# Cross-covariance attention with a gated feed-forward block: longer q-k bursts, an uneven last output tile, and a later second v tile

## Chip, cores, metric

One core of one Trainium2 chip. The metric is the device time of one execution in microseconds (us), the median of several runs. No second state of the chip is in play: all runs quoted here are of the state called fast.

## The reference

For each of 4 batches of 6016 tokens and 256 channels, channel attention makes a 256 x 256 matrix from normalized q and k, applies it to v, and a feed-forward block with a silu gate (256 to 1536 to 256) follows:

```python
def _attn_ref(q, k, v, tau):
    qn = q / (np.linalg.norm(q, axis=1, keepdims=True) + 1e-06)
    kn = k / (np.linalg.norm(k, axis=1, keepdims=True) + 1e-06)
    s = kn.transpose(0, 2, 1) @ qn / tau
    s = s - s.max(-1, keepdims=True)
    a = np.exp(s)
    a /= a.sum(-1, keepdims=True) + 1e-09
    return (v @ a).astype(np.float32)

def _moe_ref(x, w_gate, w_val, w_out):
    g = x @ w_gate
    silu = g * (1.0 / (1.0 + np.exp(-g)))
    val = x @ w_val
    return (silu * val @ w_out).astype(np.float32)
```

## The kernel before

The attention matrix is multiplied into w_gate and w_val once per batch (`Wg`, `Wv`), so that v goes straight into the feed-forward block. v comes in chunks of 512 rows; a chunk has 12 steps, and in each TensorE makes `g_ps` and `v_ps` for this chunk and two `o_new` matmuls for the one before. While one batch runs, q and k of the next are loaded, squared and multiplied in the background: `plan[step]` lists what is issued at a step. A v tile is loaded by GpSimd's queue, which casts it, into a buffer in DRAM, and SyncE's queue transposes it from there into `vT`:

```python
    def load_v(b, ci):
        ...
        vb = vb_tiles[(b * NCH + ci) % 2]
        nc.gpsimd.dma_start(
            out=vb[:mv, :].rearrange("(p s) c -> p (s c)", s=cm),
            in_=v[b, cs * P:cs * P + mv, :].rearrange("(p s) c -> p (s c)", s=cm))

    def transpose_v(b, ci):
        ...
        nc.sync.dma_start_transpose(out=vT[:, :, :mv], in_=vb[:mv, :])

    def gemm1_pair(b, t):            # the q-k product of two row blocks, fp8
        ...
        for jh in range(CH):
            js = slice(jh * P, (jh + 1) * P)
            if pm == 2:
                nc.tensor.matmul(kq[:, jh, :], q_sb[:, ps:ps + 2, js],
                                 k_sb[:, ps:ps + 2, :],
                                 start=(t == 0 and jh == 0), stop=last,
                                 perf_mode=DR, skip_group_check=True)
        ...
    # make_plan(b): two pairs at a time
            plan[step].append((norm_acc, t))
            if t % 2 == 1:
                plan[step + 1].append((gemm1_pair, t - 1))
                plan[step + 1].append((gemm1_pair, t))
    # the start, after all of batch 0's k and q; one queue, in this order
    load_first_v()
    load_w(0, HW)                    # HW = 256, WP = 512
    load_w(HW, WP)
    load_v(*allc[1])
    transpose_v(*allc[1])
    for wc in range(1, NWC):
        load_w(wc * WP, (wc + 1) * WP)
    nc.gpsimd.dma_start(out=w_out_sb, ...)
```

`load_w` loads one block of columns of w_gate and one of w_val. Behind w_out follow, in the same queue, the third v tile and the first q and k of batch 1. The end of the kernel (`finish`) makes the last 128 output rows in two halves of 128 columns, each in a tile of the pool `psum_o`, which has two.

## Time and profile before

| | before |
|---|---|
| time, median of 3 runs | 811.15 us (810.33 to 811.29) |
| same kernel, beside the changed one, 6 runs | 810.77 us (810.26 to 811.29) |
| span of the profiled run | 808.5 us |
| busy: TensorE, VectorE, ScalarE, GpSimd | 98%, 68%, 56%, 32% |

How to read the lines below and in the prediction: in the timeline a line is start, duration, engine, source line, operation, output and inputs, and a count of like instructions merged into it; a bracket at the end is idle time of the engine just before and what ended it. PE is TensorE's matmuls, PEld its weight loads, SPq and ACTq are DMA issues of SyncE and ScalarE. The line numbers are the kernel's own.

### The profile page before, as it was taken

How to read it: one execution, taken by the hardware profiler on the slowest of the kernel's cores; microseconds unless marked ns; L12 is line 12 of the kernel's file. 1: busy time of each engine (PE TensorE's matmuls, PEld its weight loads, DVE VectorE, ACT ScalarE, POOL GpSimd, SP SyncE). 2: the span in 40 equal slices, each digit the busy share in tenths (PEclk: the TensorE clock that was granted, in tenths of full speed). 3: DMA queues.
4: the chain of work that ended last, by engine and by line, in shares of the span. 5: the costliest groups of instructions: out<-in, count | busy, mean ns of one | idle time of the engine just before them, and what ended most of it. 6: DMA issues, size and time to landing. Idle time of an engine off the chain costs nothing.

```text
span 808.5 us, 11893 instructions
## 1 busy us (share of the span) xinstructions
PE 788.9 (98%) x3902; PEld 384.6 (48%) x3976; DVE 550.3 (68%) x842; ACT 454.4 (56%) x802; POOL 256.7 (32%) x314
## 2 busy tenths in 40 slices
PE   4899999999999999999999999999999999999998
PEld 3644444444454444444454444444445444444446
DVE  4777887658667878667666787756866665666654
ACT  4666666555556666555556666655555555555553
POOL 4415887422104786422000777720100000000000
PEclk9999999999999999999999999999999999999999
DMA  9996999799986885889997787569747556565543
GB/s 89 144 154 94 160 181 171 148 108 173 171 154 133 143 140 125 168 72 184 153 144 168 144 159 150 124 130 150 142 107 141 133 136 132 118 153 129 115 119 98
DMA packets 202077, 112.34 MB, mean 139 GB/s; under 512 B 149808, under 2 KB 188848, under 8 KB 201264
## 3 DMA queue, kind: packets, MB, share of 16 engines
q1 hardware_dynamic: 183968, 84.51, 44.9%
q0 software_dynamic: 17904, 27.01, 32.1%
q8 instruction: 31, 0.51, 0.3%
q14 instruction: 30, 0.25, 0.1%
q10 hardware_dynamic: 144, 0.07, 0.0%
HBM read 79.04 MB, written 60.43 MB: 172 GB/s over the span
## 4 chain that ended last, share of the span: by engine, by line
PE 95%; DMA 3%; issue 1%; ACT 0%; DVE 0%; POOL 0%; POOLq 0%
PE g_ps L447 30%; PE v_ps L447 30%; PE o_new L488 29%; PE ps L414 2%; DMA q_sb<-in_q_dram 2%; PE kq_new L168 2%; PE o_new L541 1%; DMA k_sb<-in_k_dram 1%; ACT silu L453 0%; PE last_ps L565 0%; PE ss_new L195 0%; PE unit_ps L414 0%; PE kq_new L173 0%; PE cols L218 0%; ACT pl L497 0%
## 5 line engine op out<-in xcount | busy, mean ns | idle before, releaser
L457 DVE TENSOR_TENSOR sv<-silu,v_ps 128x512 bf16<-128x512 bf16 (+1 forms) x576 | 387.2, 673 | 217.5 <-ACT silu L453 215.8
L453 ACT ACTIVATE silu<-g_ps 128x512 bf16<-128x512 f32 (+1 forms) x576 | 339.3, 589 | 294.2 <-PE g_ps L447 249.4
L447 PE MATMUL v_ps<-vT,Wv 128*128 128x512 bf16 (+1 forms) x1107 | 325.9, 374 | 1.2
L447 PE MATMUL g_ps<-vT,Wg 128*128 128x512 bf16 (+1 forms) x1105 | 325.7, 375 | 1.2
L488 PE MATMUL o_new<-sv,w_out_sb 128*128 128x512 bf16 (+1 forms) x1079 | 319.2, 375 | 1.3
L447 PEld LDWEIGHTS <-Wv 128*128 128x128 bf16 x1152 | 112.7, 98 | 131.0 <-ACT Wv L426 0.4
L300 POOL TENSOR_TENSOR acc_new<-acc_new,sq 128x512 f32<-128x512 f32 x135 | 156.2, 1157 | 55.2 <-DVE sq L290 40.7
L488 PEld LDWEIGHTS <-w_out_sb 128*128 128x128 bf16 x1104 | 108.0, 98 | 126.4
L447 PEld LDWEIGHTS <-Wg 128*128 128x128 bf16 x1152 | 109.6, 98 | 122.2 <-DVE Wv L424 0.2
L126 POOL DMA_DIRECT2D vb_new<-in_v_dram x47 | 24.2, 514 | 259.1 <-DMA vT<-vb_new 257.9
L498 DVE COPY pl<-o_new 128x512 uint16<-128x512 uint16 (+1 forms) x92 | 62.6, 680 | 16.9 <-ACT pl L497 16.6
L290 DVE TENSOR_TENSOR sq<-q_sb 128x512 bf16<-128x512 fp8e5 x72 | 65.7, 912 | 0.0
L497 ACT COPY pl<-o_new 128x512 uint16<-128x512 uint16 (+1 forms) x92 | 53.1, 577 | 18.9 <-PE o_new L488 17.9
L291 ACT ACTIVATE sq<-k_sb 128x512 bf16<-128x512 fp8e5 x72 | 44.2, 614 | 0.0
L168 PE MATMUL kq_new<-k_sb,q_sb 128*128 128x512 fp8e5 x184 | 34.5, 312 | 1.7 <-DMA q_sb<-in_q_dram 1.7
L111 POOL DMA_DIRECT2D q_sb<-in_q_dram x45 | 25.3, 562 | 11.7 <-DMA k_sb<-in_k_dram 9.8
L168 PEld LDWEIGHTS <-q_sb 128*128 128x256 fp8e5 x184 | 22.0, 136 | 10.0 <-DMA q_sb<-in_q_dram 2.9
L195 PE MATMUL ss_new<-sq,ones_bf 128*128 128x256 bf16 x83 | 14.6, 332 | 10.9 <-ACT sq L185 10.9
L359 POOL TENSOR_SCALAR den<-th 128x512 f32<-128x512 f32 x3 | 1.8, 615 | 73.1 <-ACT th L358 73.1
L111 POOL DMA_DIRECT2D k_sb<-in_k_dram x42 | 22.9, 547 | 2.9 <-DVE sq L290 1.7
L295 POOL TENSOR_TENSOR acc_new<-sq 128x512 f32<-128x512 bf16 x3 | 3.5, 1153 | 40.9 <-DVE sq L290 40.9
L195 PEld LDWEIGHTS <-ones_bf 128*128 128x128 bf16 x83 | 9.3, 117 | 14.8 <-issue 10.7
(96 smaller groups left out, 212.4 us busy)
## 6 DMA issues: line engine op xcount, KB each, us to landing
rows<-pl SPq DMA_DIRECT2D x86, 256.0 KB, 2.8
out_dram<-ot_new SPq DMA_DIRECT2D x43, 512.0 KB, 3.8
vb_new<-in_v_dram POOLq DMA_DIRECT2D x43, 256.0 KB, 4.9
q_sb<-in_q_dram POOLq DMA_DIRECT2D x36, 128.0 KB, 6.5
k_sb<-in_k_dram POOLq DMA_DIRECT2D x33, 128.0 KB, 7.2
ot_new<-rows SPq DMA_TRANSPOSE x92, 3.7
k_sb<-in_k_dram POOLq DMA_DIRECT2D x5, 256.0 KB, 8.9
rows<-pl SPq DMA_DIRECT2D x6, 192.0 KB, 2.4
```

What stands on the lines that cost most here:

```text
L111: nc.gpsimd.dma_start(out=dst[:, gs:gs + gm, :], in_=src[b].rearrange("(p s) c -> p s c", s=NS)[:, gs:gs + gm, :])
L126: nc.gpsimd.dma_start(out=vb[:mv, :].rearrange("(p s) c -> p (s c)", s=cm), in_=v[b, cs * P:cs * P + mv, :].rearrange("(p s) c -> p (s c)" ...
L168: nc.tensor.matmul(kq[:, jh, :], q_sb[:, ps:ps + 2, js], k_sb[:, ps:ps + 2, :], start=(t == 0 and jh == 0), stop=last, perf_mode=DR, skip_ ...
L290: nc.vector.tensor_mul(sq[:, :pm, 0, :], q_sb[:, ps:ps + pm, :], q_sb[:, ps:ps + pm, :])
L291: nc.scalar.activation(sq[:, :pm, 1, :], k_sb[:, ps:ps + pm, :], ACT.Square)
L300: nc.gpsimd.tensor_tensor(out=acc, in0=acc, in1=sq[:, s, :, :], op=ALU.add)
L447: nc.tensor.matmul(dst[:, :mv], W[:, kk, fs], vT[:, kk, :mv], start=(kk == 0), stop=(kk == CH - 1))
L453: nc.scalar.activation(silu[:, :mv], g_ps[:, :mv], ACT.Silu)
L457: nc.vector.tensor_mul(sv[:, f, :mv], silu[:, :mv], v_ps[:, :mv])
L488: nc.tensor.matmul(self.o_ps[h][:, :self.mv], w_out_sb[:, f, h * P:(h + 1) * P], self.sv[:, f, :self.mv], start=(f == 0), stop=(f == FH - 1))
L497: nc.scalar.copy(pl[:, 0, :self.mv], halves[:, 0, :self.mv])
L498: nc.vector.tensor_copy(pl[:, 1, :self.mv], halves[:, 1, :self.mv])
```

## The change

Three parts, each meant to take a little idle time from TensorE. Four pairs of the q-k product in one go instead of two; the last output rows as 192 and 64 columns, in banks that nothing else uses by then; the w blocks of columns 512 to 1023 loaded ahead of the second v tile, because a matmul waited for them.

```diff
@@ finish
-            HC = C // 2
-            for h in range(2):
-                cols = slice(h * HC, (h + 1) * HC)
-                last_ps = psum_o.tile([P, HC], FP32, tag="o")
+            for h, cols in enumerate((slice(0, 3 * C // 4), slice(3 * C // 4, C))):
+                HC = cols.stop - cols.start
+                last_ps = psum_gv.tile([P, HC], FP32, tag="gv"[h])
...
-                last_sb = opool.tile([P, HC], FP32, tag="last_sb")
+                last_sb = opool.tile([P, HC], FP32, tag="last_sb%d" % h)
@@ make_plan
-            if t % 2 == 1:
-                plan[step + 1].append((gemm1_pair, t - 1))
-                plan[step + 1].append((gemm1_pair, t))
+            if t % 4 == 3 or t == NP - 1:
+                for u in range(t - t % 4, t + 1):
+                    plan[step + 1].append((gemm1_pair, u))
@@ start
     load_w(HW, WP)
+    load_w(WP, 2 * WP)
     load_v(*allc[1])
     transpose_v(*allc[1])
-    for wc in range(1, NWC):
+    for wc in range(2, NWC):
```

## The prediction

> **What bounds the kernel now.** I read the page first, then who TensorE waited for, then single stretches of the timeline: one around a q-k product in mid-kernel, one at the start where the weights and the first v tiles land, one at the end. The page says in three lines that the kernel is TensorE from end to end:
>
> ```profile
> span 808.5 us, 11893 instructions
> ...
> PE 788.9 (98%) x3902; PEld 384.6 (48%) x3976; DVE 550.3 (68%) x842; ACT 454.4 (56%) x802; POOL 256.7 (32%) x314
> ...
> PE 95%; DMA 3%; issue 1%; ACT 0%; DVE 0%; POOL 0%; POOLq 0%
> ```
>
> The third is the chain that ended last. The view of waits has nothing for TensorE after 35 us: its waits (10.9 us for ACT's squares, 1.7 us for q) all lie in the first batch's norm, which the change doesn't touch. From 35 to 804 us matmuls of 512 columns start every 0.216 us. So a gain can only be time TensorE spends on something else than streaming, and the diff names three such places. The first is the q-k product in mid-kernel (start, duration, engine, line):
>
> ```profile
> 102.98 0.59 PE L488 MATMUL o_new<-sv,w_out_sb 128*128 128x512 bf16 x2
> 103.19 0.57 PEld L168 LDWEIGHTS <-q_sb 128*128 128x256 fp8e5 x4
> 103.22 0.79 PE L168 MATMUL kq_new<-k_sb,q_sb 128*128 128x512 fp8e5 x4
> 103.84 0.12 PEld L447 LDWEIGHTS <-Wg 128*128 128x128 bf16 x2
> 103.85 0.60 PE L447 MATMUL g_ps<-vT,Wg 128*128 128x512 bf16 x2
> ```
>
> The bf16 weight load after the fp8 burst starts at 103.84, hard against its matmul at 103.85; elsewhere it starts a whole matmul earlier. By single starts in the trace: last o_new matmul 103.193, second g_ps matmul 104.076, so 0.883 us. Streaming alone is 2 x 0.216 + 4 x 0.109 = 0.868 (0.109 is the spacing inside bursts). A switch to fp8 and back costs 0.015 us. I measured all 36 bursts of batches 1 to 3: 0.015 each, save nine that show one matmul more because a record is missing.
>
> The second place is the start:
>
> ```profile
> 39.78 0.59 PE L447 MATMUL g_ps<-vT_new,Wg 128*128 128x512 bf16 x2
> 40.00 0.10 PEld L414 LDWEIGHTS <-exT 128*128 128x128 bf16 x1
> 40.29 0.59 PE L414 MATMUL ps<-w_gate_sb,exT 128*128 128x512 bf16 x2
> ```
>
> The second of the g_ps pair starts at 39.996, so the w_gate matmul could start at 40.21; it starts at 40.29, 0.077 us late. The trace has the last part of that w_gate block (columns 512 to 1023) landing at 40.25. What lies ahead of it on GpSimd's queue is the second v tile:
>
> ```profile
> 33.01 0.54 POOL L126 DMA_DIRECT2D vb_new<-in_v_dram  x1 [1.19 <-DMA q_sb<-in_q_dram]
> 33.66 0.72 POOL L623 DMA_DIRECT2D w_gate_sb<-in_moe_w_gate_dram  x1
> 34.38 0.70 POOL L623 DMA_DIRECT2D w_val_sb<-in_moe_w_val_dram  x1
> ...
> 49.91 0.51 POOL L126 DMA_DIRECT2D vb_new<-in_v_dram  x1 [10.12 <-DMA vT<-vb_new]
> ```
>
> ```profile
> 38.98 1.34 SPq L135 DMA_TRANSPOSE vT<-vb_new  x1
> ```
>
> ```profile
> 51.94 0.59 PE L447 MATMUL g_ps<-vT,Wg 128*128 128x512 bf16 x2
> ```
>
> The v tile lands at 38.96, its transpose is issued at 38.98, first packets 42.95, last packet 48.53, landing 49.37, first use at 51.94: slack 2.6 us. This is the number that the third part of the change spends.
>
> The third place is the end:
>
> ```profile
> 803.98 0.83 PE L565 MATMUL last_ps<-w_out_sb,sv 128*128 128x128 bf16 x12
> ```
>
> ```profile
> 804.18 0.59 ACT L550 COPY o_sb<-o_new 128x512 f32<-128x512 f32 x1 [2.89 <-PE o_new L541]
> 804.80 0.37 SPq L553 DMA_DIRECT2D out_dram<-o_sb  x1
> 804.85 0.27 ACT L570 COPY last_sb<-last_ps 128x128 f32<-128x128 f32 x1
> 805.15 0.37 ACTq L571 DMA_DIRECT2D out_dram<-last_sb  x1
> 805.69 0.29 DVE L573 COPY last_sb<-last_ps 128x128 f32<-128x128 f32 x1 [3.21 <-PE last_ps L565]
> 806.01 0.34 SPq L574 DMA_DIRECT2D out_dram<-last_sb  x1
> ```
>
> The twelve matmuls of the first half start 0.056 apart, the last at 804.60; the second half begins at 804.82, 0.17 us late, because its bank (two in that pool) is still read by ACT's o_sb copy until 804.77.
>
> **What the Trainium skill says.** "TensorE: Matmul & The Clock Gate", section "Weight-path perf modes": DoubleRow turns the fast weight load off and its weight load is 72% dearer. The trace: 136 ns against 98, 39% more, yet bursts still run at 0.109 us, so that load is hidden. The same page, "Step-by-step: what each phase is for": weight loads are pulled ahead of running matmuls; the trace agrees except at the burst's end, as shown. "DMA: Bandwidth & Descriptors", section "Queues, rings and completion order": each DMA engine takes turns between the queues that have work, by packet. The trace agrees: while the transpose ran, both queues moved some 240 packets per us.
>
> **The change part by part.**
>
> q-k product: the same 184 DoubleRow matmuls, and the instruction order shows only that the bursts become 8 long. In batches 1 to 3 there are 24 pairs each, so 12 bursts become 6; 3 x 6 x 0.015 = 0.27 us saved, all on the path. The first batch has bursts of 8 already and runs them at 0.109 us, so a longer burst costs nothing in itself. While it runs (0.87 us) ACT and DVE get no new g tile; they are 56% and 68% busy and catch up.
>
> Weights: the two w blocks move ahead of v, and land earlier by v's share of the queue (w_val before it lands 37.73, v 38.96: 1.23 us). The late 0.077 us goes: 0.08 saved. The w_val block had 0.5 us of slack and needs none of it.
>
> Second v tile: it now lands where w_val did, 41.53, i.e. 2.57 us later. Of the 2.57 us of slack at the use (51.94 less 49.37) nothing is left, if all else shifts rigidly. It doesn't. Estimate from the trace: issue 41.55, first packet 3.7 to 4.0 later (so it was here and at the next transpose, under a loaded queue), 45.4. By then w_out, 1536 packets from 42.6 at about 300 to 370 per us alone, has 500 to 700 packets left; shared at 240 per us they take 2.1 to 2.9 us and as many of the transpose's 1056 packets go with them, until about 48. Then comes the third v tile, beside which transposes moved some 200 packets per us later in the trace, about 2 us: 350 to 550 left become 0 to 200 at 50. Those run beside q, at some 92 per us: last packet between 49.8 and 51.8, landing 0.8 later, 50.6 to 52.6. The use stands at 51.86 now. So 0 to 0.8 us of new wait for TensorE; I book 0.2.
>
> End: 128 columns take 56 ns and 256 take 109, so by interpolation 192 take 82 and 64 take 29. First part: last start 804.89, end 805.14; second without the wait: last start 805.30, end 805.49, against 805.65. DVE's copy shrinks from 0.29 to about 0.23, so the last store is issued at 805.75 in place of 806.01 and, at its 1.5 us to landing, ends 0.26 earlier. But ACT's store of the wide part leaves at 805.51, 0.36 later than now; at its present 2.0 us it would land at 807.5, as the last one does now. I take it that it partly waited behind the o_sb store, whose packets ran until 806.47 while its own began at 806.43, and book 0.2 saved between 0.05 and 0.3.
>
> Sum: -0.27 - 0.08 + 0.2 - 0.2 = -0.35 us, 0.04%.
>
> **The rivals.** First, the transpose falls behind the whole queue (w_out, third v, q, k) and comes at 53: TensorE waits 1 us or more at 52 us and the change costs: about 811.8. For it speaks the second transpose, which took 10 us to land beside q and k; against it, that w_out is still there for half of it. Second, the longer burst starves ACT and DVE or holds back the sums into the accumulators: six bursts a batch at several 0.1 us would be 5 us, about 816. Against it: no wait of TensorE in the middle, and norms whose squares are not moved. Third, the fp8 bursts cost more than I can see, say by stretching the weight loads around them; then halving them saves 1 us or more: 809.5. Against it: the sums over single starts close to a nanosecond.
>
> **Range and chances.** The three runs span 810.33 to 811.29 and their mean is 810.9; from median and mean, less 0.35, I take 810.6. Half the range is the scatter of the runs (0.5 either way), the rest the transpose on the upper side. 2% is 16 us; no part is a tenth of it.
>
> **What would show it.** The gap over each burst of 8 should be 2 x 0.216 + 8 x 0.109 + 0.015 = 1.32 us. No wait before the w_gate matmul at 40.2. A line "g_ps ... DMA vT<-vb_new" near 52 us, or its absence, decides the v term. At the end the 24 last matmuls should follow each other without the 0.17 us gap, with ACT's store now landing last or level. I am wrong if TensorE shows waits after 55 us, if the bursts are spaced other than 0.109 us, or if the start up to 35 us moves.

## The result

| | before | changed |
|---|---|---|
| median, 6 runs each | 810.77 us | 816.78 us |
| lowest to highest | 810.26 to 811.29 | 815.06 to 817.02 |
| span of the profiled run | 808.5 us | 814.5 us |

The ratio is 1.0071 (95% interval 1.0058 to 1.0084): the mean time of the changed kernel's fast runs over that of the other's of the same rounds, so not quite the ratio of the medians above. The change costs 6 us. It is far outside the noise, and the prediction of 810.6 us was wrong by 6.2 us.

### Where the time went

The page of the changed kernel, the lines that answer to those of before:

```profile
span 814.5 us, 11893 instructions
...
PE 790.8 (97%) x3902; PEld 386.2 (47%) x3976; DVE 550.8 (68%) x842; ACT 454.4 (56%) x802; POOL 257.3 (32%) x314
...
PE 91%; DMA 6%; ACT 1%; issue 1%; POOL 0%; DVE 0%; POOLq 0%
```

The instruction counts are the same; DMA's share of the chain that ended last has doubled. The view of waits of TensorE after 34 us was empty before. Now it has one line (engine, line, waited for, total, times, longest):

```profile
PE g_ps L447 <- DMA vT<-vb_new: 4.7, 1, 4.7
```

The timeline of TensorE around it in the changed kernel:

```profile
51.40 0.59 PE L447 MATMUL v_ps<-vT_new,Wv 128*128 128x512 bf16 x2
56.69 0.60 PE L447 MATMUL g_ps<-vT,Wg 128*128 128x512 bf16 x2 [4.70 <-DMA vT<-vb_new]
57.13 0.88 PE L447 MATMUL v_ps<-vT,Wv 128*128 128x512 bf16 x2
57.80 1.06 PE L488 MATMUL o_new<-sv,w_out_sb 128*128 128x512 bf16 x2
...
60.98 0.59 PE L447 MATMUL g_ps<-vT,Wg 128*128 128x512 bf16 x2
```

The second chunk's first matmul starts at 56.69 and not at 51.94. By single starts TensorE starts nothing for 5.075 us where 0.216 is usual: 4.86 us lost. From the third line on look at the durations: pairs of matmuls that take 0.59 us elsewhere take up to 1.06. The view by stretches shows why (columns: stretch, length, busy time and count of PE, PEld, DVE, ACT, POOL, then granted clock, DMA share, GB/s); the changed kernel:

```profile
50.00:57.00 7.00, 2.30 (x12) 0.88 (x10) 2.40 (x4) 1.67 (x3) 0.00 (x0) 1.00 0.80 94
57.30:60.70 3.40, 3.40 (x9) 1.22 (x8) 0.71 (x2) 1.19 (x2) 2.56 (x5) 0.50 0.68 94
```

and the kernel before:

```profile
50.00:57.00 7.00, 7.00 (x34) 3.23 (x33) 4.56 (x7) 4.11 (x7) 2.56 (x5) 1.00 1.02 119
57.30:60.70 3.40, 3.35 (x16) 1.57 (x16) 2.02 (x4) 1.98 (x4) 0.00 (x0) 1.00 1.18 130
```

In 3.4 us soon after the wait (it ends at 56.69) the granted clock is 0.50, and 9 matmuls run where 16 did. The excess of the matmul spacing over 0.216 from 56.69 to 60.98 adds up to 1.70 us. TensorE is busy 100% of that stretch: a reader who looks at busy shares alone misses it. The six timed runs of the changed kernel have a granted clock of 0.992 to 0.996 over the whole span, the profiled run of the kernel before 0.998, so each of the six ran at a lower mean clock than that one; where in the span isn't known for the five that have no trace here.

The sum of the two traces, in four stretches:

| stretch | before, us | changed, us | difference |
|---|---|---|---|
| start to the second chunk's first g_ps | 51.94 | 56.69 | +4.75 |
| from there to the first last_ps matmul | 752.04 | 753.47 | +1.43 |
| from there to the last landing | 3.57 | 3.44 | -0.13 |
| from there to the end of the span | 0.93 | 0.94 | 0.00 |

The first is 4.86 of wait, less 0.08 that the earlier weights gave at 40.2 us, less 0.03 by which the changed kernel was already ahead at 36.4 us, where both still do the same. The second is 1.70 of slow clock less 0.27, which is the shorter q-k product. They add to 6.05, and the spans, to two places, are 814.54 and 808.49. So nothing of the loss is left over for the bursts or the end.

### Why the transpose came late

The issues on GpSimd's queue in the changed kernel, the one on SyncE's, and the chain that ended last in this stretch (start, length, what):

```profile
33.00 0.70 POOL L623 DMA_DIRECT2D w_gate_sb<-in_moe_w_gate_dram  x1 [0.94 <-DMA q_sb<-in_q_dram]
33.69 0.71 POOL L623 DMA_DIRECT2D w_val_sb<-in_moe_w_val_dram  x1
34.40 0.54 POOL L126 DMA_DIRECT2D vb_new<-in_v_dram  x1
...
57.21 0.51 POOL L126 DMA_DIRECT2D vb_new<-in_v_dram  x1 [17.45 <-DMA vT<-vb_new]
```

```profile
41.52 1.35 SPq L135 DMA_TRANSPOSE vT<-vb_new  x1
```

```profile
34.40 7.10 DMA vb_new<-in_v_dram
41.50 0.02 issue
41.52 15.13 DMA vT<-vb_new
56.65 0.05 issue
56.69 0.60 PE g_ps L447 x2
```

The v tile lands at 41.50 and the transpose is issued at 41.52, 2.53 us later than before. But it lands 15.13 us after its issue, where it took 10.4 before: 7.3 us later at the end. The delay was multiplied on the way. I counted from the trace how many packets had started (before: of the transpose and of w_out; changed: also of what lies behind):

| time, us | before: transpose of 1024 | before: w_out of 1536 | changed: transpose | changed: w_out | changed: third v of 16 | changed: q and k of 256 |
|---|---|---|---|---|---|---|
| 45 | 465 | 546 | 0 | 827 | 0 | 0 |
| 47 | 942 | 1023 | 316 | 1386 | 0 | 0 |
| 48 | 1019 | 1309 | 352 | 1422 | 1 | 0 |
| 50 | 1024 | 1536 | 520 | 1524 | 14 | 30 |
| 52 | 1024 | 1536 | 688 | 1536 | 16 | 165 |
| 53 | 1024 | 1536 | 929 | 1536 | 16 | 212 |
| 54 | 1024 | 1536 | 987 | 1536 | 16 | 232 |
| 55 | 1024 | 1536 | 1019 | 1536 | 16 | 247 |

Before, the transpose begins at 42.95 and has w_out's 512-byte packets for company all the way: both move about 238 packets per us, packet for packet, and it is through while w_out still has 227 packets to go. In the changed kernel w_out has had the engines alone for 3 us when the transpose begins at 45.53, and two thirds of it are gone. From 46 to 47 the two move about 225 packets per us each, as before. Then the cheap company ends with 708 of 1024 packets still to come. From 47 to 48 nearly nothing moves on either queue: packets that started near 47.0 took about 0.95 us where 0.03 to 0.06 is usual. (Before has such a pause too, at 47.8 us, when the transpose needs only five packets more. I have no cause for it. In both traces a 16 KB packet of the queue that the page lists as "q8 instruction" starts 0.74 us ahead of the pause; many others of that queue have no pause behind them.) From 47 to 50, over w_out's rest and the third v tile, 204 packets go, 68 per us. From 50 to 52, beside q and k, 84 per us: a q packet takes 0.172 us, a transpose packet 0.031. With no company at all the engines did 977 in the us from 61 to 62 in the kernel before. I read this so: the transpose's end is tied to the end of the queue that it shares. The last part of k lands at 56.61 and the transpose at 56.65.

The queue itself ends later, too. The sixteen parts of w_out landed between 49.8 and 50.5 us before, and between 48.5 and 53.3 in the changed kernel: the sixteen DMA engines fell out of step, and while the slow ones worked off q and k the others had nothing. The stretch 50 to 57 shows it as a DMA share of 0.80 against 1.02. Packet records don't carry their engine here, so what slowed those engines stays open.

This spread bears on the transpose itself, and it is a rival to q and k as the cause of the tail. The transpose's sixteen parts landed between 49.27 and 49.37 us before. In the changed kernel thirteen landed between 55.31 and 55.45, and the last three at 55.88, 56.49 and 56.65. The packet starts tell the same: from 52 to 53 us 241 packets went, but the last 37 started between 54.0 and 55.2. So at least the last 1.2 us belongs to a few late engines, and TensorE needs all sixteen parts.

A second instance, in the kernel before itself, fits the reading by queue: its next transpose, issued at 51.62 with q and k of batch 1 in the queue, landed at 61.8, after 10.2 us, and only when the queued k had landed at 61.1. It was needed at 67.5 us, so nobody waited. In the changed kernel the same transpose was issued at 53.90 and landed at 57.73: by then q and k were almost through.

### The other two parts

The q-k product in the changed kernel:

```profile
108.94 0.59 PE L488 MATMUL o_new<-sv,w_out_sb 128*128 128x512 bf16 x2
109.16 1.01 PEld L168 LDWEIGHTS <-q_sb 128*128 128x256 fp8e5 x8
109.19 1.22 PE L168 MATMUL kq_new<-k_sb,q_sb 128*128 128x512 fp8e5 x8
110.25 0.12 PEld L447 LDWEIGHTS <-Wg 128*128 128x128 bf16 x2
110.25 0.60 PE L447 MATMUL g_ps<-vT,Wg 128*128 128x512 bf16 x2
```

From the last o_new to the second g_ps it is 1.320 us by single starts, 0.015 over streaming, in 14 of the 18 bursts; the other four show one missing record (1.536). That is the number foretold for a burst of 8.

The end:

```profile
810.37 0.59 ACT L550 COPY o_sb<-o_new 128x512 f32<-128x512 f32 x1 [2.89 <-PE o_new L541]
811.36 0.32 ACT L570 COPY last_sb<-last_ps 128x192 f32<-128x192 f32 x1 [0.40 <-PE last_ps L565]
811.71 0.37 ACTq L571 DMA_DIRECT2D out_dram<-last_sb  x1
811.71 0.23 DVE L573 COPY last_sb<-last_ps 128x64 f32<-128x64 f32 x1 [3.04 <-PE last_ps L565]
811.96 0.34 SPq L574 DMA_DIRECT2D out_dram<-last_sb  x1
```

The 24 matmuls follow each other at 82 ns (192 columns) and 29 ns (64) with no gap between the halves; the wait of 0.17 us for the bank is gone. The wide store lands at 813.44 and the narrow one at 813.61.

### The profile page after: what moved, and what is told of

The parts are those of the page before. It is cut to its first block, busy times and chain, and to the rows that moved or that the text cites. A ratio compares the mean times of both kernels' runs of the same rounds, so it can differ in the third digit from the quotient of the medians.

```text
span 814.5 us, 11893 instructions
## 1 busy us (share of the span) xinstructions
PE 790.8 (97%) x3902; PEld 386.2 (47%) x3976; DVE 550.8 (68%) x842; ACT 454.4 (56%) x802; POOL 257.3 (32%) x314
## 4 chain that ended last, share of the span: by engine, by line
PE 91%; DMA 6%; ACT 1%; issue 1%; POOL 0%; DVE 0%; POOLq 0%
PE g_ps L447 29%; PE v_ps L447 29%; PE o_new L488 28%; DMA q_sb<-in_q_dram 2%; PE ps L414 2%; DMA vT<-vb_new 2%; PE kq_new L168 2%; DMA k_sb<-in_k_dram 2%; PE o_new L541 1%; DMA vb_new<-in_v_dram 1%; ACT silu L453 1%; POOL k_sb L111 0%; DVE sv L457 0%; PE last_ps L565 0%; ACT pl L497 0%
## 5 line engine op out<-in xcount | busy, mean ns | idle before, releaser
L168 PE MATMUL kq_new<-k_sb,q_sb 128*128 128x512 fp8e5 x184 | 29.2, 301 | 1.0 <-DMA q_sb<-in_q_dram 1.0
L414 PEld LDWEIGHTS <-exT 128*128 128x128 bf16 x104 | 9.9, 98 | 10.8
```

The lines of the kernel that those rows point to most:

```text
L168: nc.tensor.matmul(kq[:, jh, :], q_sb[:, ps:ps + 2, js], k_sb[:, ps:ps + 2, :], start=(t == 0 and jh == 0), stop=last, perf_mode=DR, skip_ ...
L414: nc.tensor.matmul(ps, state[b, "exT"][:, jh, ih * P:(ih + 1) * P], (w_gate_sb, w_val_sb)[w][:, jh, cols], start=(jh == 0), stop=(jh == CH ...
```

## Experiments

None gave a result, so everything here rests on the two traces and the twelve timed runs. What was asked, and would have told the theories apart, was this.

Third part alone, on the kernel before:

```diff
     load_w(HW, WP)
+    load_w(WP, 2 * WP)
     load_v(*allc[1])
     transpose_v(*allc[1])
-    for wc in range(1, NWC):
+    for wc in range(2, NWC):
```

> The kernel before with the third part alone (second v tile behind the w blocks of columns 512 to 1023); the q-k bursts stay at 4 matmuls and the end at two halves. Theory A (the whole loss is the late second v tile): a wait of TensorE for the transposed v near 52 us of 4 to 5.5 us as in the changed kernel, then one stretch of half clock (3.4 us), and a time of 0.3 to 0.6 us above the changed kernel, because the gains of the two other parts are missing: about 817.2. Rival B (the longer q-k bursts cost, or the three parts together): under 814, with no wait over 1 us near 52 us.

Not run. The third part undone, on the changed kernel (the same diff the other way round):

> The changed kernel with the third part undone: bursts of 8 and the 192/64 end remain, the second v tile is back in its old place. Theory A: no wait of TensorE for the transposed v, and 0.27 us (18 switches of 15 ns) plus 0.13 us (end) under the kernel before: 810.4 where before is 810.8, ratio about 0.9995. Rival B: 814 to 817, as the changed kernel.

Not run. Dummy matmuls in the wait:

```diff
+            if gi == 1 and f == 0:
+                keep_warm(22)
             us = range(2 * f, 2 * f + 2) if gi == 0 ...
```

> The changed kernel with 22 matmuls of 512 columns on constant data in front of the second chunk's first product, 22 x 0.216 = 4.75 us, which fill the wait for the transposed v and whose result nobody reads. Theory A1 (the wait costs twice: 4.9 us of idle and, because the clock is halved for 3.4 us after it, 1.7 us more): the clock stays at full speed after 57 us, matmuls there start every 0.216 us, and the time is 1.7 us less, about 815.1. Rival A2 (the slow matmuls after the wait have another cause, such as the transfers then under way, or the halving comes anyway): they stay at 0.43 us apart to about 60.7 us and the time stays at 816.8 or rises.

Not run. The first q and k of the next batch moved behind the load that waits for the transpose:

```diff
-            step = 9 + 5 * g if b == 1 else 7 + 10 * (g - 7)
+            step = max(13, 9 + 5 * g) if b == 1 else 7 + 10 * (g - 7)
```

> The changed kernel with the first q and k loads of the next batch moved behind the fourth v tile's load, which waits for the transposed v, so that they no longer share the DMA engines with the transpose; w_out and the third v tile still do. Theory C (the transpose is slow because its tail runs beside q and k, whose packets take 0.17 us each): it lands at 50 to 52.5 us and not at 56.6, the wait is 0 to 0.8 us, and the time is 810.4 to 811.2. Rival D (it is slow because the engines fell out of step while w_out and the third v tile ran, or for its late issue alone): it still lands after 54 us, wait over 2 us, time over 813.

Not run. The replacement in the twins:

```diff
-            if pm == 2:
-                nc.tensor.matmul(kq[:, jh, :], q_sb[:, ps:ps + 2, js],
-                                 k_sb[:, ps:ps + 2, :],
-                                 start=(t == 0 and jh == 0), stop=last,
-                                 perf_mode=DR, skip_group_check=True)
-            else:
-                nc.tensor.matmul(kq[:, jh, :], q_sb[:, ps, js], k_sb[:, ps, :],
-                                 start=(t == 0 and jh == 0), stop=last,
-                                 skip_group_check=True)
+            nc.tensor.matmul(kq[:, jh, :], q_sb[:, ps, js], k_sb[:, ps, :],
+                             start=(t == 0 and jh == 0), stop=last,
+                             skip_group_check=True)
```

> A twin of the kernel before: the double-row mode of the q-k product, which the chip service holds back for now, is replaced by a plain fp8 matmul of the same 256 output columns on the first row block of each pair, in the same number and order (the result is wrong on purpose: every second row block is missing from the product). In the profile before, the plain fp8 matmuls of the last pair start 109 to 120 ns apart, double-row ones 109 ns. So the twin should keep the timing: about 810.6 against 810.8, no wait for the transposed v. If it is over 1 us away, experiments on the twins only hold between twins.

Not run either.

What this leaves: that the wait for the transposed v and the slow stretch after it hold the whole difference is read from the traces, where the four stretches add up. That only the third part moves the v tile is read from the diff; no kernel with that part alone was timed. That q and k, rather than the late issue by itself or the engines that fell out of step, make the tail of the transpose is argued from packet rates and not shown. That the halved clock comes from the idle time is argued from its place and the page cited below, not shown by a kernel in which one is there without the other.

## Why the prediction was wrong

**q-k bursts: right.** 0.27 foretold, 0.27 found, at the spacing foretold. (The prediction counts nine bursts with a missing record in the trace before; there are six.)

**Weights: right.** 0.08 foretold, 0.08 found; the w_gate matmul starts at 40.18 in step with its neighbour at 39.75.

**End: right, size off.** 0.2 foretold between 0.05 and 0.3; 0.13 found to the landing. The wide store did land 1.73 us after its issue and not 2.0, as assumed; but the narrow one took 1.65 where it had taken 1.55 before.

**Second v tile: the step that failed**, in two places.

The wait was booked as "0 to 0.8 us of new wait for TensorE; I book 0.2". The issue (41.55 foretold, 41.52 found) and the first packet (45.4 and 45.53) were right, and w_out had 514 packets left at 45.5, inside "500 to 700". Wrong was what came next: "Then comes the third v tile, beside which transposes moved some 200 packets per us later in the trace, about 2 us: 350 to 550 left become 0 to 200 at 50." At 48 there were 672 left, because of the pause, and at 50 still 504. From 47 to 50 the rate was 68 and not 200 per us. The 200 was taken from stretches in mid-kernel where v had no other company on its queue. The 504 then met q and k at 84 per us (92 was foretold), which is where, as I read it, the queue's end becomes the transpose's end. (By the prediction's own figures 550 less 2 x 200 leaves 150 and not 200; that changes little.) The first rival named this mechanism, "the transpose falls behind the whole queue", with the right witness, the second transpose of the kernel before; I gave it 53 us, although the k of that queue landed at 54.07 before, and argued it away with "w_out is still there for half of it". Half was not enough, and the queue ended 2.5 us later than before.

The second failure is a term that the sum doesn't have. A wait of 4.9 us is not worth 4.9 us: the clock cost 1.70 more. The rival with the wait of "1 us or more" has no such term either. The Trainium skill states it, in "TensorE: Matmul & The Clock Gate", section "Part 1: The HAM clock gate": the clock gate looks at windows of 3413 ns and lets half the pulses through after at least one idle window. The trace agrees on length and rate: a record of half clock, 3.413 us long, begins 0.6 us after the wait's end, and matmuls in it start every 0.427 us, not 0.216. The estimate from that page, half of 3.41, is 1.71, against 1.70 found. On the condition the traces say more than that sentence: each kernel has another such record, also 3.413 us long, in the first batch's norm (from 16.85 us before, from 19.76 us changed), and there no idle time of TensorE since its first matmul had been longer than 1.32 and 1.04 us. So a shorter wait is not sure to go free.

The bookkeeping was therefore right in every term that is counted from TensorE's own instructions and wrong in the one that had to be simulated by hand through shared DMA engines; the range treated that term as if its error were as small as the others'.

## What to carry to other kernels

Slack of a transfer is not spent one for one. A transpose delayed by 2.5 us came 7.3 us later; by the packet counts it had lost the cheap transfers it used to run beside and met expensive ones. So ask not only when it is issued but what will be in the queue beside it until it ends, and as a cautious guess put its landing at the end of that queue: two transposes here landed 0.03 and 0.70 us after it. And 0.08 us to be won on one wait was bought with the only slack of a load that everything behind it needs: look first at what the new last in the queue is for, and add a slow clock, 1.70 us here, to a wait of this size.

## What the Trainium skill lacked or had wrong

- "DMA: Bandwidth & Descriptors", section "Queues, rings and completion order", states the turns between queues but no rates for a transpose beside other traffic. Here: 977 packets of 256 bytes per us alone, 225 to 240 beside 512-byte packets, 84 beside q and k.
- The same page, "Latency and other measured facts", gives about 600 ns to the first byte for issues from SyncE's or ScalarE's queue. Under a loaded queue the transposes' first packet started 3.8 to 4.0 us after the issue in three cases; with an idle queue 1.3 us (issue 63.37, packet 64.67 in the kernel before).
- "TensorE: Matmul & The Clock Gate", section "Weight-path perf modes", has the double-row weight load 72% dearer; here it is 39% (136 against 98 ns). No page gives the price of a switch from fp8 double-row to bf16 and back: 15 ns, the same for bursts of 4 and of 8.
